# The mixing stage of a talking-heads attention and Fourier kernel: three engines in emission order, work dealt to steps by a table, maxima in halves, folding in small operations

## The chip, the cores and the metric

The kernel runs on one core of a Trainium2 chip. The metric is the device time of one execution in microseconds (us); lower is better. TensorE is called PE in the profile (its weight loads PEld), VectorE is DVE, ScalarE is ACT, GpSimd is POOL, SyncE is SP.

## The reference, cut to what matters

```python
scores = np.matmul(q, k.transpose(0, 1, 3, 2)) / np.sqrt(64)      # 8 batches, 12 heads, 448 x 448
scores = np.einsum('bhij,hg->bgij', scores, w_pre)                # premix: heads into heads
attn = np.exp(scores - np.max(scores, axis=-1, keepdims=True))
attn = attn / (np.sum(attn, axis=-1, keepdims=True) + 1e-09)
attn = np.einsum('bhij,hg->bgij', attn, w_post)                   # postmix
x = np.matmul(attn, v)          # then (8, 448, 12 * 64) = (8, 448, 768)
X = np.fft.fft(np.fft.fft(x, axis=1), axis=2)
u = x + np.real(X)
un = (u - mean(u)) / np.sqrt(var(u) + 1e-6)
out = u + np.maximum(un @ w_ch1, 0.0) @ w_ch2                     # 768 -> 3072 -> 768
```

Everything up to `u` is the mixing stage. The last two lines are the second stage; the change doesn't touch it.

## The kernel before

The mixing stage is a loop of 192 steps, 24 for each batch. A step mixes the heads of some twenty query rows (448 / 24 = 18.7). Its fixed part is the premix (eight matrix products, four for each half of its tile), a maximum, two exponentials, a scaling, the postmix and the transposition `Pv` of its result ("the turn"). Beside that, steps carry other products: scores of later rows (QK), attention times value (AV), transposes of q and k, transposes of x, and the two Fourier transforms of the previous batch (`emit_z`, `emit_s2`). These come from queues, `fill`, in which each entry has a step at which it is due.

```python
def emit_premix(T):
    mx = pmx.tile([P, 2, 512], F32, name="mx", tag="mx")      # one buffer, two PSUM banks
    ...                                                       # 4 products into half 0, 4 into half 1
def emit_max(T):                                              # VectorE: one maximum over both halves
    nc.vector.tensor_reduce(nmx[:, :], steps[T]["mx"][:, :, :S], axis=AX.X, op=ALU.max, negate=True)
def emit_exp(T):                                              # ScalarE
    for x in range(2):
        nc.scalar.activation(PP[:, x, :], steps[T]["mx"][:, x, :S], ACTF.Exp,
                             bias=steps[T]["nmx"][:, x:x + 1], accum_out=den[:, x:x + 1])
def emit_scale(T):                                            # GpSimd, with a reciprocal on VectorE
    nc.gpsimd.tensor_scalar(den[:, :], den[:, :], 1e-9, None, op0=ALU.add)
    nc.vector.reciprocal(out=rcp[:, :], in_=den[:, :])
    for x in range(2):
        nc.gpsimd.tensor_scalar(PP[:, x, :], PP[:, x, :], rcp[:, x:x + 1], 1.0, op0=ALU.mult, op1=ALU.mult)
def emit_turn(T):                                             # VectorE: transposes what postmix left in po
    nc.vector.transpose(g["Pv"]..., steps[T]["po"][:, :, :S])
...
# emit_s2, second transform: its product goes to one of four PSUM buffers `ms`;
# four VectorE additions to X then read that buffer and set it free
...
def fold(g):                                                  # GpSimd, for each pair of row groups
    nc.gpsimd.tensor_tensor(xs[:n, :], Xa[:n, :], Xb[:n, :], op=ALU.add)
    nc.gpsimd.tensor_tensor(xd[:n, :], Xa[:n, :], Xb[:n, :], op=ALU.subtract)
    ...                                                       # xe from xs, xo from xd: inputs of emit_z
...
with tc.manual_schedule(engines={mybir.EngineType.PE, mybir.EngineType.DVE}):
    while s < TOT or any(fill.values()):
        take("none", s)                                       # loads
        emit_premix(s + LM); emit_max(s + LM); emit_exp(s + LM)      # LM = 2
        flush()                                               # evacuations left from the step before
        take("tile", s)                                       # AV and QK products, between premix and postmix
        emit_postmix(s)
        ... wts.deal(1)                                       # one weight conversion on VectorE, in most steps
        emit_turn(s)
        emit_scale(s + LM)
        emit_gather(s + LG)                                   # SyncE: gathers Kr from the scores Sb, LG = 4
        take("full", s)                                       # transposes, transforms
        s += 1
```

`manual_schedule` names the engines whose instructions keep the order in which they are emitted. On the others the framework's scheduler chooses. PSUM evacuations were dealt to ScalarE or VectorE by a running estimate of each one's load (`_Evac`).

Of the kernel before, what the change touches and what calls it, by code (L numbers as in the profile page):

```python
# [61 lines left out]

NC = 6
# [47 lines left out]


class _Evac:


    def __init__(self, nc):
        self.nc = nc
        self.a = 0.0
        self.d = 0.0

    def pick(self, n):
        ca, cd = 165.0 + n * 0.833, 150.0 + n * 1.042
        if self.a + ca <= self.d + cd:
            self.a += ca
            return "a"
        self.d += cd
        return "d"

    def copy(self, out, in_, n):
        if self.pick(n) == "a":  # L130
            self.nc.scalar.copy(out=out, in_=in_)  # L131
        else:
            self.nc.vector.tensor_copy(out=out, in_=in_)

    def negate(self, out, in_, n):
        if self.pick(n) == "a":
            self.nc.scalar.mul(out, in_, -1.0)
        else:
            self.nc.vector.tensor_scalar(out, in_, -1.0, None, op0=ALU.mult)

    def relu(self, out, in_, n):
        if self.pick(n) == "a":
            self.nc.scalar.activation(out, in_, ACTF.Relu)
        else:
            self.nc.vector.tensor_scalar(out, in_, 0.0, None, op0=ALU.max)
# [127 lines left out]
def mix_phase(ctx, tc, ident, q, k, v, w_pre, w_post, u_scr, wts):  # L273
# [8 lines left out]
    praw = pool("praw", 3)  # L282
# [18 lines left out]
    ev = _Evac(nc)  # L301
    pend = []
# [45 lines left out]
    def emit_load_qk(b, xx):  # L348

        for nm, src in (("q", q), ("k", k)):  # L350
            t = praw.tile([P, C7, 2, D], F32, name="raw" + nm, tag="raw")
            for y in range(2):
                for x in range(2):
                    nc.gpsimd.dma_start(
                        out=t[64 * y:64 * y + 64, :, x, :],
                        in_=src[b, 6 * y + 2 * xx + x].rearrange(
                            "(p c) d -> p c d", c=C7))
            batches[b]["raw" + nm, xx] = t
        return []

    def emit_load_v(b):
        t = pvv.tile([P, 6, C7 * D], F32, name="vv", tag="vv")
        for y in range(2):
            nc.gpsimd.dma_start(
                out=t[64 * y:64 * y + 64, :, :],
                in_=v[b, 6 * y:6 * y + 6].rearrange("h (p c) d -> p h (c d)", c=C7))
        batches[b]["v"] = t
        return []


    def emit_xpose(b, xx, nm):
# [10 lines left out]
        for c0, n in ((0, 4), (4, 3)):  # L382
# [11 lines left out]
            evs.append(lambda dst=dst, src=src, n=n: ev.copy(dst, src, n * P))  # L394
        return evs

    def emit_qk(n, xx):
# [7 lines left out]
        for y in range(2):  # L405
            lo = r0 + MG * y
            for x in range(2):
# [5 lines left out]
        return [lambda x=x: ev.copy(bk["Sb"][:124, 2 * xx + x, :], pss[x][:124, :S], S)  # L413
                for x in range(2)]
# [24 lines left out]
    def emit_max(T):  # L439
        nmx = psm.tile([P, 2], F32, name="nmx", tag="nmx")  # L440
        nc.vector.tensor_reduce(nmx[:, :], steps[T]["mx"][:, :, :S], axis=AX.X,  # L441
                                op=ALU.max, negate=True)
        ev.d += 1084.0
        steps[T]["nmx"] = nmx

    def emit_exp(T):
# [6 lines left out]
        ev.a += 1656.0  # L453
        steps[T]["PP"], steps[T]["den"] = PP, den

    def emit_scale(T):
        PP, den = steps[T]["PP"], steps[T]["den"]
        nc.gpsimd.tensor_scalar(den[:, :], den[:, :], 1e-9, None, op0=ALU.add)
        rcp = psm.tile([P, 2], F32, name="rcp", tag="rcp")
        nc.vector.reciprocal(out=rcp[:, :], in_=den[:, :])  # L460
        ev.d += 150.0
# [17 lines left out]
    def emit_turn(T):  # L479
# [7 lines left out]
        ev.d += 1084.0  # L487
        steps[T].clear()

    def emit_av(g, pr):  # L490
# [6 lines left out]
        for jb in range(C7):  # L497
            for x in range(2):
                for y in range(2):
# [3 lines left out]
                        st["v"][64 * y:64 * y + 64, i, jb * D:(jb + 1) * D],  # L503
# [9 lines left out]
        def done(y):  # L513
            rs = _row(pss[y])
            eng = ev.pick(160 + 60)
            for e in range(2):
# [5 lines left out]
                if eng == "a":  # L522
                    nc.scalar.copy(out=dst, in_=src)
                else:
                    nc.vector.tensor_copy(out=dst, in_=src)
        evs = [lambda y=y: done(y) for y in range(2)]
        if pr == 2 and back:

            o = MG if g["gi"] == 1 else MG + GR
            evs.append(lambda: nc.gpsimd.memset(XT[:, :, o:o + 1], 0.0))  # L530
        pend.extend(evs)
        return []

    def emit_x(g):
# [5 lines left out]
        for u in range(2):  # L540
            ps = ms_tile()
            for i in range(3):
                nc.tensor.transpose(ps[:n, i * P:(i + 1) * P],
                                    XT[:, 3 * u + i, MG:MG + n], ident[:, :])
            evs.append(lambda u=u, ps=ps: ev.copy(X[:n, u * DH:(u + 1) * DH],
                                                  ps[:n, :DH], DH))
        if g["gi"] % 2:
            evs.append(lambda: fold(g))
        return evs

    def fold(g):
# [4 lines left out]
        xs = pxs.tile([GR + 1, DM], F32, name="xs", tag="xs")  # L556
        xd = pxs.tile([GR + 1, DM], F32, name="xd", tag="xd")
        nc.gpsimd.tensor_tensor(xs[:n, :], Xa[:n, :], Xb[:n, :], op=ALU.add)
        nc.gpsimd.tensor_tensor(xd[:n, :], Xa[:n, :], Xb[:n, :], op=ALU.subtract)
        xe = pxf.tile([GR + 1, DH + 1], F32, name="xe", tag="xe")  # L560
        xo = pxf.tile([GR + 1, DH - 1], F32, name="xo", tag="xo")
        nc.gpsimd.tensor_copy(out=xe[:n, 0:DH + 1:DH], in_=xs[:n, 0:DH + 1:DH])
        nc.gpsimd.tensor_tensor(xe[:n, 1:DH], xs[:n, 1:DH], xs[:n, DM - 1:DH:-1],
                                op=ALU.add)
        nc.gpsimd.tensor_tensor(xo[:n, :], xd[:n, 1:DH], xd[:n, DM - 1:DH:-1],
# [400 lines left out]
```

## Time and profile before

| | before |
|---|---|
| time, median of 3 (range) | 2651.92 us (2649.42 to 2665.38) |
| span of the profiled run, mean granted clock | 2652.4 us, 0.980 |
| first premix product | 46.77 us |
| from there to the first product of step 189 | 950.4 us |
| the rest (last steps, second stage) | 1655.2 us |

The page's first part gives busy time, share of the span and number of instructions of each engine:

```profile
PE 2454.0 (93%) x18544; PEld 1575.4 (59%) x18544; DVE 1514.2 (57%) x2842; ACT 723.5 (27%) x1989; POOL 660.0 (25%) x1129
```

Two lines of the waits were not used in the prediction; here they are for 200 to 900 us. The columns of a list of waits are: engine, its line and what it makes, whom it waited for; then us in total, times, longest us.

```profile
DVE Pv L484 <- PE po L473: 95.0, 67, 4.3
...
DVE rcp L460 <- POOL den L458: 72.8, 43, 4.8
```

VectorE stood 95 us at the turn, waiting for the postmix to end, and 72.8 us at the reciprocal, waiting for GpSimd to add 1e-9 to the sums `den`. VectorE is not the busiest engine, so both lines look harmless. The timeline tells them apart, by what they do to the next maximum. Count over batches 1 to 6, 144 steps. In 41 of them the turn, after a wait, began only 0.18 us after the next premix had begun, and still the maximum began 1.26 us after that premix on average, where 1.13 is usual: the late turn cost 0.13. But 33 maxima began more than 1.4 us after their premix, and before 29 of them VectorE's last wait was the one at the reciprocal. One of these steps begins with its premix at 393.18 and lasts 5.22 us, for 4.09 of products:

```profile
395.76 0.17 DVE L460 RECIPROCAL rcp<-den 128x2 f32<-128x2 f32 x1 [1.50 <-POOL den L458]
395.84 1.07 DVE L441 TENSOR_REDUCE nmx<-mx 128x2 f32<-128x896 f32 x1
...
398.40 1.15 PE L434 MATMUL mx<-Kr,kw 60*64 60x448 f32 x8 [1.05 <-ACT PP L450]
```

The bracket is idle time before, and what ended it. GpSimd made the sum late, the reciprocal held the maximum, the maximum the exponentials, and these the next premix. Where the next premix followed the exponentials at once (within 0.35 us), steps with this wait lost 29.4 of the 97.6 us that these six batches lose. The change moves that addition to VectorE.

### The profile page before, as it was taken

How to read it: one execution, taken by the hardware profiler on the slowest of the kernel's cores; microseconds unless marked ns; L12 is line 12 of the kernel's file. 1: busy time of each engine (PE TensorE's matmuls, PEld its weight loads, DVE VectorE, ACT ScalarE, POOL GpSimd, SP SyncE). 2: the span in 40 equal slices, each digit the busy share in tenths (PEclk: the TensorE clock that was granted, in tenths of full speed). 3: DMA queues.
4: the chain of work that ended last, by engine and by line, in shares of the span. 5: the costliest groups of instructions: out<-in, count | busy, mean ns of one | idle time of the engine just before them, and what ended most of it. 6: DMA issues, size and time to landing. Idle time of an engine off the chain costs nothing.

```text
span 2652.4 us, 47290 instructions
## 1 busy us (share of the span) xinstructions
PE 2454.0 (93%) x18544; PEld 1575.4 (59%) x18544; DVE 1514.2 (57%) x2842; ACT 723.5 (27%) x1989; POOL 660.0 (25%) x1129
## 2 busy tenths in 40 slices
PE   4889899899999885988899999999999999999999
PEld 2344444444444343665677777777777777777776
DVE  2666666666666664677646654665566356733333
ACT  2655555555555541211111111111111111111111
POOL 5565555556565532111000000000000000000000
PEclk8989999999999997999999999999999999999999
DMA  5453545444444433823264445443545354454331
GB/s 154 137 148 125 153 125 158 136 139 153 139 149 143 143 123 110 284 93 136 83 206 125 137 145 174 131 149 103 182 140 160 128 161 127 138 164 131 119 119 55
DMA packets 154141, 372.99 MB, mean 141 GB/s; under 512 B 21959, under 2 KB 75207, under 8 KB 153920
## 3 DMA queue, kind: packets, MB, share of 16 engines
q1 hardware_dynamic: 123360, 260.63, 29.8%
q0 software_dynamic: 30560, 109.34, 14.2%
q8 instruction: 148, 2.42, 0.4%
q14 instruction: 73, 0.60, 0.1%
HBM read 212.96 MB, written 74.34 MB: 108 GB/s over the span
## 4 chain that ended last, share of the span: by engine, by line
PE 74%; DVE 9%; POOL 5%; DMA 4%; ACT 3%; issue 2%; SPq 1%; POOLq 0%; ACTq 0%; DVEq 0%
PE psP L818 16%; PE psP L867 15%; PE psR L818 8%; PE psR L867 7%; PE mx L434 4%; PE psQ L818 4%; PE ms L501 4%; PE po L473 4%; PE psQ L867 4%; PE ms L408 3%; DMA Kr<-Sb 2%; PE ms L589 2%; ACT PP L450 2%; DVE nmx L441 2%; PE ms L575 2%
## 5 line engine op out<-in xcount | busy, mean ns | idle before, releaser
L867 PE MATMUL psP<-w2t,h 128*128 128x384 f32 x1344 | 464.2, 489 | 1.9 <-DVE u L873 1.9
L818 PE MATMUL psP<-ub,w1t 128*128 128x256 f32 x2016 | 463.5, 379 | 0.0
L818 PEld LDWEIGHTS psP<-ub,w1t 128*128 128x128 f32 x2016 | 383.1, 190 | 61.0 <-ACT ub L793 0.3
L867 PEld LDWEIGHTS psP<-w2t,h 128*128 128x128 f32 x1344 | 255.6, 191 | 170.5 <-DVE u L873 3.7
L450 ACT ACTIVATE PP<-mx,nmx 128x448 f32<-128x448 f32 x384 | 239.9, 629 | 408.2 <-DVE nmx L441 404.8
L202 POOL DMA_DIRECT2D raw<-in_moe_w_ch_dram x120 | 69.3, 577 | 923.6 <-DVE tmp L241 904.7
L484 DVE STREAM_TRANSPOSE Pv<-po 128x896 f32<-128x896 f32 x192 | 213.6, 1112 | 131.7 <-PE po L473 131.2
L463 POOL TENSOR_SCALAR PP<-PP,rcp 128x448 f32<-128x448 f32 x384 | 246.4, 652 | 132.3 <-DVE rcp L460 124.7
L441 DVE TENSOR_REDUCE nmx<-mx 128x2 f32<-128x896 f32 x192 | 207.5, 1081 | 119.4 <-PE mx L434 118.1
L873 DVE TENSOR_TENSOR u<-u,psP 128x384 f32<-128x384 f32 x336 | 182.5, 553 | 144.5 <-PE psP L867 141.9
L434 PE MATMUL mx<-Kr,kw 60*64 60x448 f32 x1536 | 198.0, 574 | 49.0 <-ACT PP L450 34.2
L823 ACT COPY h<-psP 128x512 f32<-128x512 f32 x42 | 24.6, 585 | 767.9 <-PE psP L818 767.9
L818 PE MATMUL psR<-ub,w1t 128*128 128x256 f32 x1008 | 231.3, 379 | 0.0
L867 PE MATMUL psR<-w2t,h 128*128 128x384 f32 x672 | 230.5, 486 | 0.0
L408 PE MATMUL ms<-kT,qT 64*64 64x448 f32 (+1 forms) x1536 | 205.4, 554 | 12.0 <-DVE X L602 11.3
L818 PEld LDWEIGHTS psR<-ub,w1t 128*128 128x128 f32 x1008 | 191.5, 190 | 26.0
L829 DVE TENSOR_TENSOR h<-h,psQ 128x512 f32<-128x512 f32 x42 | 28.9, 688 | 299.5 <-PE psQ L818 293.8
L501 PEld LDWEIGHTS ms<-Pv,vv 64*64 64x64 f32 x5376 | 161.0, 136 | 62.3 <-issue 37.1
L473 PE MATMUL po<-PP,kw 60*32 60x448 f32 x3072 | 193.6, 562 | 2.8 <-DVE rcp L460 2.3
L501 PE MATMUL ms<-Pv,vv 64*64 64x120 f32 x5376 | 172.5, 271 | 15.8 <-ACT Sb L131 15.4
L867 PEld LDWEIGHTS psR<-w2t,h 128*128 128x128 f32 x672 | 127.2, 190 | 87.4
L131 ACT COPY Sb<-ms 124x448 f32<-124x448 f32 x296 | 146.9, 537 | 32.9 <-DMA Kr<-Sb 12.6
(93 smaller groups left out, 2685.1 us busy)
## 6 DMA issues: line engine op xcount, KB each, us to landing
ub<-ub SPq DMA_DIRECT2D x294, 384.0 KB
Kr<-Sb SPq DMA_DIRECT2D x768, 105.0 KB
raw<-in_moe_w_ch_dram POOLq DMA_DIRECT2D x72, 256.0 KB, 3.2
raw<-in_moe_w_ch_dram POOLq DMA_DIRECT2D x48, 384.0 KB, 3.9
w<-wst POOLq DMA_DIRECT2D x18, 896.0 KB, 4.7
w<-wst POOLq DMA_DIRECT2D x12, 1344.0 KB, 6.3
w1t<-w SPq DMA_DIRECT2D x42, 384.0 KB
w2t<-w SPq DMA_DIRECT2D x42, 384.0 KB
```

The lines of the kernel that those rows point to most:

```text
L131: self.nc.scalar.copy(out=out, in_=in_)
L408: nc.tensor.matmul(pss[x][64 * y:64 * y + r0 + 64 - lo, :S], st["qT", xx][64 * x:64 * x + 64, y, lo:r0 + 64], st["kT", xx][64 * x:64 * x + ...
L434: nc.tensor.matmul(mx[64 * z:64 * z + 64, x, :S], kw1[64 * x:64 * x + KR, :], Kr[64 * x:64 * x + KR, z, :], start=True, stop=True)
L441: nc.vector.tensor_reduce(nmx[:, :], steps[T]["mx"][:, :, :S], axis=AX.X, op=ALU.max, negate=True)
L450: nc.scalar.activation(PP[:, x, :], steps[T]["mx"][:, x, :S], ACTF.Exp, bias=steps[T]["nmx"][:, x:x + 1], accum_out=den[:, x:x + 1])
L463: nc.gpsimd.tensor_scalar(PP[:, x, :], PP[:, x, :], rcp[:, x:x + 1], 1.0, op0=ALU.mult, op1=ALU.mult)
L473: nc.tensor.matmul(po[o:o + 32, z, :S], kw2[64 * z:64 * z + KR, y, :], PP[64 * z:64 * z + KR, :, c * HS:(c + 1) * HS], start=True, stop=True)
L484: nc.vector.transpose(g["Pv"][:, T % GT, :].rearrange("p (z s) -> p z s", z=2), steps[T]["po"][:, :, :S])
L501: nc.tensor.matmul(pss[y][64 * x:64 * x + 64, :nu * R], st["v"][64 * y:64 * y + 64, i, jb * D:(jb + 1) * D], _ap(Pv, 64 * y * rp + 32 * jb ...
L818: nc.tensor.matmul(p[:, m, :], w1[i][:, kc, m * P:(m + 1) * P], ub[:, kc, :], start=i in OPENS and m == kc == 0, stop=kc == NK - 1, skip_g ...
L867: nc.tensor.matmul(p, lhs[i][:, kf, x * P:(x + 1) * P], w2[i][:, kf, :], start=i in OPENS and kf == 0, stop=kf == FM - 1, skip_group_check ...
L873: nc.vector.tensor_tensor(us_, us_, p, op=ALU.add)
```

## The change

Its intent is that PE never waits in a full batch. PE, VectorE and ScalarE keep emission order. A table says at which step each piece of extra work comes. AV products move behind the postmix, QK products behind the scaling. The maximum is taken half by half, so that the first exponential can start early. GpSimd's folding is cut into six small operations, one a step, and the addition of 1e-9 goes to VectorE. Who evacuates what is fixed (`ENG`).

```diff
+AT_T = ((7, 0), (18, 18), (15, 17))
+AT_QK = ((0, 2, 2), (0, 1, 2), (0, 1, 2), (0, 1, 2),
+         (0, 1, 2), (1, 1, 2), (0, 1, 2), (0, 1, 2))
+AT_AV = ((0, 2, 4), (0, 1, 4), (3, 4, 5), (2, 3, 4))
+AT_X = (11, 20, 25, 29)
+AT_Z = (38, 38, 38, 38, 42, 42, 42)
+AT_S = ((41, 44), (49, 53))
+ENG = {("tr", "q", 4): "d", ("tr", "q", 3): "a", ("tr", "k", 4): "a",
+       ("tr", "k", 3): "d", "QK": "aa", "AV": "aa", "X": "aa", "z": "a"}
 ...
-    praw = pool("praw", 3)
+    praw = pool("praw", 4)
 ...                                  # q and k loaded one at a time, v in three parts
     def emit_max(T):
-        nc.vector.tensor_reduce(nmx[:, :], steps[T]["mx"][:, :, :S], axis=AX.X,
-                                op=ALU.max, negate=True)
+        for x in range(2):
+            nc.vector.tensor_reduce(nmx[:, x:x + 1], steps[T]["mx"][:, x, :S],
+                                    axis=AX.X, op=ALU.max, negate=True)
 ...
     def emit_scale(T):
-        nc.gpsimd.tensor_scalar(den[:, :], den[:, :], 1e-9, None, op0=ALU.add)
-        nc.vector.reciprocal(out=rcp[:, :], in_=den[:, :])
+        nc.vector.tensor_scalar(rcp[:, :], den[:, :], 1e-9, None, op0=ALU.add)
+        nc.vector.reciprocal(out=rcp[:, :], in_=rcp[:, :])
 ...
+        folds.extend([lambda: pairs(ALU.add, 0), lambda: pairs(ALU.add, 1), even,
+                      lambda: pairs(ALU.subtract, 0), lambda: pairs(ALU.subtract, 1),
+                      odd])
 ...
-    with tc.manual_schedule(engines={mybir.EngineType.PE, mybir.EngineType.DVE}):
+    with tc.manual_schedule(engines={ET.PE, ET.DVE, ET.Activation}):
         while s < TOT or any(fill.values()):
             take("none", s)
             if 0 <= s + LM < TOT:
                 emit_premix(s + LM)
                 emit_max(s + LM)
+            flush()
+            if 0 <= s + LM < TOT:
                 emit_exp(s + LM)
-            flush()
-            take("tile", s)
             if 0 <= s < TOT:
                 emit_postmix(s)
-                if s >= 4 and s % GS not in (13, 19, 0, 1):
-                    wts.deal(1)
+            take("AV", s)
+            if 0 <= s < TOT:
                 emit_turn(s)
+            if s >= 4:
+                wts.deal(1)
             if 0 <= s + LM < TOT:
                 emit_scale(s + LM)
+            if folds:
+                folds.pop(0)()
+            take("QK", s)
             if 0 <= s + LG < TOT:
 ...
                 emit_gather(s + LG)
             take("full", s)
             s += 1
```

## The prediction

> **What bounds the kernel now.** I read the page first, then the busy times by stretch, then step lengths from the timeline, then the waits and the chain of the mixing stage. The page says TensorE (PE) is busy 93% of 2652.4 us. That figure mixes two stages. In the stretches of the mixing stage (0 to about 1000 us) PE shows 85 to 93 busy us per 100; after 1400 us it shows 1200.00 busy in 1200. The second stage is not touched by the change and has nothing to give except at its start. So the question is the mixing stage: 192 steps, 24 for each of 8 batches.
>
> A step begins with the first premix product (line 434). The timeline of one step that runs tight (523 to 528 us) and of one that does not (532 to 538 us) shows what PE work costs and what waits cost. First the chain of waits there, whose pieces are time from piece to piece and so show throughput without pipeline tails (start, duration, what):
> ```profile
> 523.27 0.75 PE ms L408 x8
> 524.02 0.91 PE po L473 x16
> 524.93 2.78 PE ms L589 x8
> 527.71 0.91 PE mx L434 x8
> ...
> 530.29 2.13 PE ms L589 x6
> ...
> 543.68 1.52 PE ms L501 x51
> ```
> So, when PE is fed: premix 0.91, postmix 0.91, score products 0.75 us (2.57 for the three, needed in nearly every step), attention-times-value products 1.52, second transform 2.78 (even) or 2.13 (odd). By the same reading two first transforms take 1.72 (0.86 each) and six X transposes 0.91; steps with two sets of seven input transposes last 4.61 to 4.66, so one set is (4.66 - 2.57)/2, about 1.06 us. Steps with score and value products need 2.57 + 1.52 = 4.09, and the tight ones last 4.06 to 4.10. Now the one that does not (timeline; the bracket is idle time before, and who ended it):
> ```profile
> 532.35 0.98 PE L434 MATMUL mx<-Kr,kw 60*64 60x448 f32 x8
> ...
> 533.48 1.09 DVE L441 TENSOR_REDUCE nmx<-mx 128x2 f32<-128x896 f32 x1 [0.69 <-PE mx L434]
> ...
> 535.87 0.55 DVE L602 TENSOR_TENSOR X<-X,ms 112x383 f32<-112x383 f32 x1
> ...
> 536.48 0.97 PE L408 MATMUL ms<-kT,qT 64*64 64x448 f32 x6 [0.93 <-DVE X L602]
> ...
> 538.29 0.98 PE L434 MATMUL mx<-Kr,kw 60*64 60x448 f32 x8
> ```
> It lasts 538.29 - 532.35 = 5.94 for the same 4.09 of products: two score products stood in the queue because their PSUM tile was still being added to X by VectorE (DVE), which first had to do the maxima of this step. The lost 1.85 is more than the bracketed 0.93, because products already started are counted busy while they drain.
>
> I did this for all steps from the first premix (46.77 us) to 997: they last 950 us, their products need 803, so 147 us are lost. Six full batches (1 to 6) last 730 in place of 634: 121.7 against 105.7 each, 16 lost. The losses sit in fixed places of the 24: step 13 (3.3 us, value products waiting for ScalarE (ACT) evacuations), 5 (2.8), 19 (2.5), 6 (1.75), 1 (1.5), 18 (1.1), 21 (0.9). Steps with little beside the basic products last 3.71 to 3.82 for up to 3.48 of work: there the loop premix, maximum, exponentials, next premix bounds, since the premix tile has one buffer. The waits between 200 and 1000 us agree:
> ```profile
> DVE nmx L441 <- PE mx L434: 87.9, 73, 3.4
> ...
> PE mx L434 <- ACT PP L450: 20.5, 32, 2.0
> ...
> PE ms L501 <- ACT Sb L131: 15.4, 7, 2.2
> ...
> PE ms L385 <- ACT Sb L131: 13.3, 11, 5.2
> ...
> PE ms L408 <- DVE X L602: 11.3, 11, 1.4
> ```
> **What the Trainium skill says.** "Perfetto Trace Analysis", Identifying the Most-Contended Engine, calls matmul busy share a bad measure of headroom because matmuls are pipelined; this trace agrees, PE reads as 91% busy in a batch (110.58 of 121.20 us from 347.04 to 468.24) whose products need 105.7/121.2 = 87%. "TensorE: Matmul & The Clock Gate", head table, gives ScalarE and VectorE strictly first-in-first-out queues: the order of emission decides what waits, which is how the 5.94 us step came about. "PSUM — Partial Sum Buffer", PSUM bank collisions, forbids two engines in one bank at once; the two halves of the premix tile are 512 floats each, a bank each, so a maximum of half 0 beside products of half 1 is allowed (before, one maximum reads both, so no trace shows it yet). "SBUF — State Buffer", Who interferes with whom, says that VectorE's two-port modes and GpSimd exclude each other; the trace agrees: the 128x256 mask of line 219 took 0.28 us at 74.63 and 1.08 at 540.54, while GpSimd scaled from 540.22 for 1.25. One such conversion a step stays as it was.
>
> **The change part by part.**
> *Work.* PE products are the same, 105.7 us a batch. Maxima in halves: 24 x 1.09 becomes 48 of some 0.55, no more than 1 us a batch. The 1e-9 addition moves from GpSimd (0.215 each) to DVE (about 0.1 each). All evacuations except half of the input transposes go to ACT: 24 x 2 of 0.45, value copies 12 x 0.5, X 8 x 0.4, z 7 x 0.31, inputs about 4, with 24 x 1.24 of exponentials, some 67 us of 106. DVE has about 80 us. Neither becomes the bound on average.
> *The loop premix to premix.* It is 3.76 to 3.82 now. The first exponential waits for 0.54 less, so about 3.2; if the first half may start before the second half's products, 2.8. The table leaves no step of a full batch below 3.32 us of products (I summed each of the 24: 3.32 to 4.09 for most, 5.6 to 6.5 in steps 1, 5, 14, 17, 18, 20). So in a full batch PE sets the pace in each step and the loop has slack.
> *PSUM waits.* Every second transform is now followed in its step by transposes, whose emission flushes its four DVE additions before the next maxima. In step 1: transform over at 5.35, additions (4 x 0.47, plus 0.2) at 7.45, next maximum due at 6.26 + 1.1 = 7.36, value products at 8.08. Practically no wait where 1.85 was lost. Steps 13, 18, 19 lose their waits the same way (3.3, 1.1, 2.5), as does the exponential wait in 21 and 22.
> *GpSimd.* Folding in pieces of 0.9 to 1.3 us, one a step, replaces runs of 1.82 + 1.80 + 0.18 + 1.0 + 1.0. But steps 9 to 11 hold three loads of four issues (0.73 each, 8.8) plus scaling 3 x 1.25 plus folding about 3, or 15.5 us against 10.9 of PE: it falls behind by about 4.6, and the scaling has about 3.6 of slack before its postmix. I charge 1 to 2 us a batch for that.
> *Sum.* Batches 1 to 6: 3.5 lost in place of 16, from all residues; 6 x 12.5 = 75. Batches 0 and 7, which lack products to fill with and lose 19 and 24: 8 and 10, saves 25. The four steps around the start: 5 less. Together about 105.
> *Ends.* The first premix waits until 46.77 with 10.4 us for its gather; four input buffers in place of three and fewer loads ahead of it: 5 us less, an estimate with little under it. At the end PE waits 6.63 for the fold and then SyncE for the weight store:
> ```profile
> 1044.59 6.79 DMA w<-wst
> ...
> 1053.64 6.38 DMA u<-u
> ```
> Conversions are now dealt in every step from 4 on (188 for 160 operations, where 158 were dealt before), so the store is long done: up to 6.8 saved if the final write of X doesn't take its place, and 3 to 4 from even folds first. I take 8.
> Total 105 + 5 + 8 = 118, so 2534. I give back 11 for what the sums cannot see, and predict 2545.
>
> **Rivals.**
> (1) GpSimd takes over: it is busy 70.5 of 121.2 us in the batch above; squeezed into 107 us and with loads bunched it may hold up postmix more than I charged. For: chain pieces on folding and scaling already exist (xs 1.82, xd 1.78). Against: pieces are now small. Worth 3 to 5 us a batch: 2570 to 2580.
> (2) The gathers (Kr): SyncE issues four of 0.767 a step, 3.07 of 4.4 us, and the score buffer waits for them to land (ACT waited 4.61 at 308 to 313 us). For: pace rises by 12%. Against: evacuations into it now come a step later, and PE waited for gathers only 8.9 us from 200 to 1000. If it binds: 2580 to 2600.
> (3) Strict order on ACT puts evacuations ahead of the exponentials of the same step and stalls when one is late. Against: these evacuate products issued before the premix. If wrong in the full steps: gain halves, 2595.
> (4) Nothing new binds and losses vanish: 803 plus some 15, 2505.
>
> **Range and chances.** Because product times are fixed to about 0.03 us a step, the floor is firm: 2500. The upside of the time is open to (1) to (3), singly likely mild. Range 2505 to 2598. Faster by over 2% means below 2599: 0.91. Within 2%: 0.08. Slower: 0.01.
>
> **What would show it.** Steps with value and score products at 4.09 nearly everywhere; batch period 107 to 111; second stage unchanged (36.2 us a tile in the steady part); products waiting for X additions or Sb copies close to gone; no w store on the chain at the end. Wrong if batches last over 115: then PE waits, read before postmix (GpSimd), before premix (gathers or exponentials), or before value products (ACT order), tell which rival it is.

## The result, and the profile after

| | before | after |
|---|---|---|
| time, median (range), 4 runs each | 2654.11 us (2649.42 to 2665.38) | 2546.99 us (2544.47 to 2549.62) |
| span and clock of the profiled run | 2652.4 us, 0.980 | 2542.7 us, 0.991 |
| first premix product | 46.77 us | 49.14 us |
| from there to step 189 | 950.4 us | 844.8 us |
| the rest | 1655.2 us | 1648.8 us |
| a full batch (mean of 1 to 6), of it lost | 121.68, 16.35 | 108.07, 3.20 |
| lost in batch 0, batch 7 | 19.4, 24.1 | 13.2, 6.3 |

The ratio is 0.9591, with a 95% interval of 0.9557 to 0.9624. A ratio here is the mean time of one kernel's runs over the mean of the other's in the same rounds, so it isn't quite the ratio of the medians. The three parts of the profiled spans add up: +2.4 - 105.6 - 6.4 = -109.7 us, the difference of the spans. "Lost" is the length of a step less what its products need when fed, summed; the needs are good to some 0.1 us, and step 18 reads 0.68 too little in every kernel with the new table.

First the page of the kernel after:

```profile
PE 2418.8 (95%) x18544; PEld 1552.7 (61%) x18544; DVE 1522.3 (60%) x3159; ACT 769.7 (30%) x2056; POOL 638.0 (25%) x1001
```

PE runs the same 18544 products. Its busy time fell by 35 us although its work didn't change: most of that must be stalls inside products, and some may be a slower clock (below). In the pages' fifth parts a half maximum costs 619 ns where one over both halves cost 1081, so the pair is dearer.

The chain around a second transform (start, duration, what), the place that stalled score products before:

```profile
552.58 0.91 PE po L460 x16
553.49 0.91 PE ms L397 x8
554.40 2.78 PE ms L582 x8
557.18 0.77 PE ms L374 x7
557.94 0.91 PE mx L423 x8
```

PE goes from one product to the next without a piece of any other engine in between. That step, from its premix at 551.63 to the next at 557.87, takes 6.24 us, where the single costs of before sum to 6.41. Step after step of the full batches reads like this. The timeline of the same moment shows why nothing waits:

```profile
557.21 0.56 DVE L593 TENSOR_TENSOR X<-X,ms 112x385 f32<-112x385 f32 x1 [1.42 <-PE ms L582]
...
558.61 0.55 DVE L595 TENSOR_TENSOR X<-X,ms 112x383 f32<-112x383 f32 x1
...
559.08 1.15 DVE L431 TENSOR_REDUCE nmx<-mx 128x1 f32<-128x448 f32 x2
```

The additions that free the transform's PSUM buffer begin the moment it ends and are over before VectorE takes the next maxima. Before, they came after the maximum, and the buffer stayed taken.

The waits of the kernel after from 200 to 900 us, the lines that answer to those of before:

```profile
PE po L460 <- POOL PP L450: 7.4, 12, 1.3
PE mx L423 <- ACT PP L439: 7.3, 16, 1.8
...
PE ms L397 <- DVE kT L283: 6.0, 6, 1.0
...
DVE Pv L471 <- PE po L460: 2.3, 5, 1.1
```

Score products no longer wait for additions to X, nor value products for evacuations of the scores. What is left is a postmix waiting for GpSimd's scaling, and a score product in step 19 waiting for an evacuation of kT. VectorE's 95 us at the turn have become 2.3, and no line with a reciprocal that waits for GpSimd is left.

And the chain at the join of the stages:

```profile
938.93 3.44 DMA u<-X,rows
```

The store of a weight tile is gone from the chain. The last write of X now stands in its place.

The parts of step time lost, by step of the batch (mean over batches 1 to 6):

| step | before | after |
|---|---|---|
| 13 (value products for evacuations) | 3.29 | about 0 |
| 5 | 2.81 | about 0 |
| 19 | 2.46 | 1.10 |
| 6, 1 | 1.75, 1.54 | about 0 |
| 18, 21 | 1.06, 0.94 | below 0, about 0 |
| 8, 23 (postmix for GpSimd) | not among the largest | 0.93, 0.59 |

One thing besides the waits differs. The granted clock of the kernel after is 1.00 in each of the eight batches; that of the kernel before is 1.00 in batches 3 and 4 alone, and 0.95, 0.97, 0.96, 0.99, 0.97 and 0.92 in batches 0, 1, 2, 5, 6 and 7. Batches 3 and 4 lose 14.4 and 13.5 us, batches 1, 2, 5 and 6 18.6, 19.8, 16.8 and 14.4. So a part of the gain may be the clock's, some 2 us a full batch (an estimate: the mean of the six, 16.3, less that of batches 3 and 4, 14.0). No run separates it, or shows why the clock differs.

### The profile page after: what moved, and what is told of

It reads as the page before. It is cut to its first block, busy times and chain, and to the rows that moved or that the text cites. A ratio compares the mean times of both kernels' runs of the same rounds, so it can differ in the third digit from the quotient of the medians.

```text
span 2542.7 us, 47627 instructions
## 1 busy us (share of the span) xinstructions
PE 2418.8 (95%) x18544; PEld 1552.7 (61%) x18544; DVE 1522.3 (60%) x3159; ACT 769.7 (30%) x2056; POOL 638.0 (25%) x1001
## 4 chain that ended last, share of the span: by engine, by line
PE 81%; DVE 7%; POOL 5%; DMA 3%; ACT 2%; issue 2%; SPq 0%; ACTq 0%; POOLq 0%; DVEq 0%
PE psP L821 17%; PE psP L870 16%; PE psR L821 9%; PE psR L870 8%; PE mx L423 5%; PE ms L487 5%; PE psQ L821 4%; PE po L460 4%; PE ms L397 4%; PE psQ L870 4%; PE ms L582 3%; DVE nmx L431 2%; ACT PP L439 2%; PE ms L568 2%; POOL xs L545 2%
## 5 line engine op out<-in xcount | busy, mean ns | idle before, releaser
L431 DVE TENSOR_REDUCE nmx<-mx 128x1 f32<-128x448 f32 x384 | 221.5, 619 | 163.2 <-PE mx L423 162.8
L450 POOL TENSOR_SCALAR PP<-PP,rcp 128x448 f32<-128x448 f32 x384 | 240.8, 639 | 284.6 <-DVE rcp L448 228.1
L397 PE MATMUL ms<-kT,qT 64*60 64x448 f32 (+1 forms) x1536 | 186.8, 557 | 7.6 <-DVE kT L283 7.6
L283 ACT COPY Sb<-ms 124x448 f32<-124x448 f32 x384 | 184.2, 541 | 7.4 <-PE ms L397 5.3
L487 PEld LDWEIGHTS ms<-Pv,vv 64*64 64x64 f32 x5376 | 142.8, 132 | 69.0 <-issue 27.1
L487 PE MATMUL ms<-Pv,vv 64*64 64x120 f32 x5376 | 165.0, 268 | 0.0
```

Of the source, the lines that this page charges most:

```text
L283: (nc.scalar.copy if eng == "a" else nc.vector.tensor_copy)(out=out, in_=in_)
L397: nc.tensor.matmul(pss[x][64 * y:64 * y + r0 + 64 - lo, :S], st["qT", xx][64 * x:64 * x + 64, y, lo:r0 + 64], st["kT", xx][64 * x:64 * x + ...
L431: nc.vector.tensor_reduce(nmx[:, x:x + 1], steps[T]["mx"][:, x, :S], axis=AX.X, op=ALU.max, negate=True)
L487: nc.tensor.matmul(pss[y][64 * x:64 * x + 64, :nu * R], st["v", pr][64 * y:64 * y + 64, x, jb * D:(jb + 1) * D], _ap(Pv, 64 * y * rp + 32 ...
```

## The experiments

The theory going in: PE paces the steps after the change, and the gain comes from PSUM buffers freed in time, which needs both the table (what comes when) and the order (who does what first). The rivals: the halves of the maximum give the gain; the small folding operations do; or the fixed order of one engine alone does. A rival that was not tested is the move of the 1e-9 addition off GpSimd: every variant of the kernel after keeps it. Twelve kernels ran, all correct, each with 3 rounds; the kernel before ran beside them.

### The maxima: e1, e2, e3

e1 takes one maximum over both halves again:

```diff
-        for x in range(2):
-            nc.vector.tensor_reduce(nmx[:, x:x + 1], steps[T]["mx"][:, x, :S], axis=AX.X, op=ALU.max, negate=True)
+        nc.vector.tensor_reduce(nmx[:, :], steps[T]["mx"][:, :, :S], axis=AX.X, op=ALU.max, negate=True)
```

> The changed kernel with one maximum over both halves, as before the change. Theory A (the halves bought nothing: in the trace of the changed kernel the first exponential starts at 72.60, after both halves have ended at 72.49, and the loop of a lean step is 3.79 us as before): time within 4 us of the changed kernel's 2547, lean steps 3.72 to 3.82. Theory B (the halves shorten the loop by 0.5 as predicted, something else takes it back): lean steps go to 4.2 or more, total up by 15 us or more.

Measured: 2546.49 us (2544.84 to 2549.82), ratio 0.957 (0.9543 to 0.9598), the same as the kernel after. The halves gave nothing. The timeline of a step with little work in the kernel after shows it:

```profile
73.99 0.98 PE L423 MATMUL mx<-Kr,kw 60*64 60x448 f32 x8 [0.99 <-ACT PP L439]
...
75.12 1.16 DVE L431 TENSOR_REDUCE nmx<-mx 128x1 f32<-128x448 f32 x2 [0.71 <-PE mx L423]
...
76.39 0.64 ACT L439 ACTIVATE PP<-mx,nmx 128x448 f32<-128x448 f32 x1 [1.59 <-DVE nmx L431]
```

The first maximum starts when all eight premix products are through, and the first exponential starts at 76.39, after both maxima (75.12 + 1.16 = 76.28). Splitting an operation doesn't split the wait. But which wait? e2 gives the two results tiles of their own:

```diff
-        nmx = psm.tile([P, 2], F32, name="nmx", tag="nmx")
+        nmx = [psm.tile([P, 1], F32, name=f"nmx{x}", tag=f"nmx{x}") for x in range(2)]
...                                  # and the two places that use it
```

> The two halves of the maximum write two tiles in place of two columns of one. Theory A (the wait of the first exponential is on the tile that both maxima write): the first exponential starts about 0.55 earlier, lean steps go from 3.79 to about 3.2; sum of what lean steps lose: some 1.4 us a batch, 8 in the first and last: total down 12 to 20 us, to about 2530. Rival (ScalarE is held by what stands before the exponential in its queue, not by the maximum): lean steps stay at 3.79, total within 4 us.

Measured: 2549.66 us (2547.54 to 2550.36), ratio 0.9583 (0.9555 to 0.9611). No gain, so the shared tile of results was not what held the exponential. e3 also splits the premix tile itself, which lies in two PSUM banks, into two tiles of one bank:

```diff
-        mx = pmx.tile([P, 2, 512], F32, name="mx", tag="mx")
+        mx = [pmx.tile([P, 512], F32, name=f"mx{x}", tag=f"mx{x}") for x in range(2)]
```

> As the run with two maximum tiles, and the premix tile is two tiles of one bank each. Theory: the first maximum starts about 0.4 earlier, when its own half of the products is done, and the next step's first half of products may start after the first exponential; lean steps about 2.8, near their product time; total 2522 to 2530, some 5 below the run with two maximum tiles alone. Rival: PE sets the pace once the loop is 3.2, no more than 2 us below it.

Measured: 2533.54 us (2529.75 to 2537.21), ratio 0.9523 (0.9493 to 0.9553): some 13 us less than the kernel after by the medians. In its timeline an exponential now stands between the two maxima:

```profile
78.14 0.62 DVE L431 TENSOR_REDUCE nmx<-mx 128x1 f32<-128x448 f32 x1
...
78.86 0.63 ACT L439 ACTIVATE PP<-mx,nmx 128x448 f32<-128x448 f32 x1 [0.53 <-DVE nmx L431]
...
79.12 0.62 DVE L431 TENSOR_REDUCE nmx<-mx 128x1 f32<-128x448 f32 x1 [0.35 <-PE mx L423]
```

The second half of this premix had waited for a gather, which drew the two maxima apart. But over batches 1 to 6 the first exponential starts 0.44 us before the second maximum ends, on average, where in the kernel after and in e2 it starts 0.12 after. The waits of the compiled programs say the same. In e2 the first exponential of a step carries a wait on VectorE and PE and the second carries none, so the first one's wait must cover both maxima. In e3 each exponential has its own wait on VectorE:

```
e2:
78 L439 Activation PP,den<-mx,nmx_1181 128x448 [waits DVE_49,PE_49,Pool_49]
79 L439 Activation PP,den<-mx,nmx_1182 128x448
e3:
78 L439 Activation PP,den<-mx_1191,nmx_1197 128x448 [waits DVE_49,Pool_49]
79 L439 Activation PP,den<-mx_1192,nmx_1198 128x448 [waits DVE_49]
```

So the framework orders the accesses of two engines to a PSUM tile by the tile, not by the half or the bank.

### Table and order: e5, b1, e9, e6, e7

e5 keeps all of the kernel after, with the steps of the kernel before in the table (four of the seven first transforms one step later):

```diff
+AT_T = ((5, 5), (16, 17), (17, 18))
+AT_QK = ((0, 1, 2),) * 8
+AT_AV = ((1, 2, 3),) * 4
+AT_X = (10, 16, 22, 28)
+AT_Z = (31, 31, 32, 33, 34, 35, 35)
+AT_S = ((36, 42), (47, 48))
```

> The changed kernel's order of emission with the step table of before (first transforms moved by at most two steps, because the folding in pieces ends later). Theory T (the table makes most of the gain, by putting transposes behind each second transform and value products where there is room): full batches last 114 to 119 in place of 108, total 2600 to 2640. Rival O (the fixed order on the three engines makes it): full batches at 111 or less, total below 2575.

Measured: 2608.65 us (2599.99 to 2611.66), ratio 0.9823 (0.9794 to 0.9852). A full batch lasts 116.66 us and loses 11.3.

b1 goes the other way: the kernel before, with its order, and the new table. It loads q and k one at a time, but keeps three input buffers and loads v whole, since a fourth buffer didn't fit in SBUF there.

```diff
-            due("full", f + aq, lambda b=b, xx=xx: emit_xpose(b, xx, "q"))
+                due("full", f + a - GS, lambda b=b, xx=xx, nm=nm: emit_xpose(b, xx, nm))
...
-                due("tile", f + GT * n + GT + 1 + pr, lambda g=g, pr=pr: emit_av(g, pr))
+                due("tile", f + GT * (n + 1) + AT_AV[n][pr], lambda g=g, pr=pr: emit_av(g, pr))
```

> The kernel before with the new step table alone (inputs loaded one by one with three buffers, old order of emission, old evacuation balance, folding in one run, one maximum). Theory T (the table makes most of the gain): total 2570 to 2600, full batches 110 to 113. Rival O (the order makes it, and a table without it is worth little): total 2620 or more, full batches 117 or more.

Measured: 2622.82 us (2617.35 to 2628.05), ratio 0.9866 (0.9836 to 0.9896). Its waits from 200 to 900 us:

```profile
DVE Pv L491 <- PE po L480: 127.9, 74, 8.5
...
PE ms L508 <- DMA vv<-in_v_dram: 15.7, 6, 3.4
```

The second line is a flaw of the experiment: with the new table the whole-v load comes too late for the value products of step 6, where 5.3 us a batch are lost, 38.8 in all. So b1 understates what the table alone can give. As measured, the table alone gives 1.3%, the rest of the change 1.8%, together 4.1%. That this is more than the sum of the two isn't shown, since the flaw hides up to 1.5% (an estimate from the 38.8 us). By the expectation's own numbers b1 fell on the side of rival O, and e5 on that of theory T: neither part alone gives the gain. Steps 13, 5, 1 and 21, which lost 3.29, 2.81, 1.54 and 0.94 before, lose nothing in b1, so the table alone is enough for what was lost there. The rest of b1's loss, 12.4 us a batch, lies above all in steps 22 and 23 (3.1 and 1.6). In step 22 of all six full batches the maximum comes late behind the reciprocal, which waits for GpSimd as it did before.

The first line is the turn again, at 128 us. In b1 it does little: once in 144 steps was it the last wait before a late maximum.

e9 keeps everything after and only puts AV and QK products back between premix and postmix:

```diff
-            if 0 <= s < TOT:
-                emit_postmix(s)
             take("AV", s)
+            take("QK", s)
             if 0 <= s < TOT:
+                emit_postmix(s)
                 emit_turn(s)
```

> The changed kernel with value and score products between premix and postmix, as before, all else as changed. Theory (PE is the pace in full batches and every buffer has slack, so the place in the step hardly counts): within 8 us of 2547. Rival (the products at the end give the scaling and the evacuations time; earlier they stand in front of the postmix and wait for PSUM): full batches at 110 or more, total up 15 or more.

Measured: 2599.80 us (2597.35 to 2602.28), ratio 0.9787 (0.9758 to 0.9816). That is 53 us more than the kernel after by the medians, as much as half of the whole gain. I had expected hardly anything of it. The timeline of a step of e9 that lasts 5.48 us (190.09 to 195.57) in place of its 3.6 of products:

```profile
190.09 0.98 PE L423 MATMUL mx<-Kr,kw 60*64 60x448 f32 x8
190.27 1.12 DVE L471 STREAM_TRANSPOSE Pv<-po 128x896 f32<-128x896 f32 x1 [2.03 <-PE po L460]
...
192.93 1.13 DVE L431 TENSOR_REDUCE nmx<-mx 128x1 f32<-128x448 f32 x2
...
194.18 0.64 ACT L439 ACTIVATE PP<-mx,nmx 128x448 f32<-128x448 f32 x1 [2.91 <-DVE nmx L431]
```

VectorE works in emission order, and the turn of a step stands ahead of the maximum of the next. With the products in front of it the postmix ends late, the turn waits (2.03 idle), and then the maxima start 2.84 us after the premix, where 1.1 is usual (73.99 to 75.12 above). The exponentials are late by that, and so is the next premix, which needs the one premix tile free. In e9's waits from 200 to 900 us VectorE stands 150.4 us at the turn, and PE 42.7 us before the premix (7.3 in the kernel after). With the postmix directly behind the premix, the turn's data is ready while the AV and QK products still run. The step is no exception: of 70 maxima that come late in batches 1 to 6 (over 1.4 us after their premix), 69 have the wait at the turn as VectorE's last.

But e9 isn't the order of before. There a late turn cost the maximum 0.13 us, because only the reciprocal stood between the two; the weight conversion stood ahead of the turn, in the time of its wait. Since the change the conversion stands behind the turn. In 57 steps of e9 a turn that waited until after the next premix had begun is followed by a conversion (0.48 us on average), the addition of 1e-9 and the reciprocal, and the maximum begins 2.01 us after the premix, 0.88 later than usual. In the step above the addition alone took 0.97 us (at 191.84), as GpSimd folded beside it. So the 53 us are what the early postmix is worth in the new order of VectorE, and not a loss that the kernel before had. No run put the conversion back ahead of the turn.

e6 emits the second transform after the transposes of its step, not before them:

```diff
-    def due(kind, at, fn):
-        fill[kind].append((at, len(fill[kind]), fn))
+    def due(kind, at, fn, late=0):
+        fill[kind].append((at, len(fill[kind]) + late, fn))
...
-                    lambda b=b, pair=pair, par=par: emit_s2(b, pair, par))
+                    lambda b=b, pair=pair, par=par: emit_s2(b, pair, par), 10000)
```

> The changed kernel with each second transform after the transposes of its step in place of before them, so that its additions are emitted after the next maxima. Theory (the PSUM tile that the additions hold is what stopped PE before): in the steps after a second transform (2, 6, 18, 21 of 24) 0.5 to 2 us lost each where 0 is lost now, 3 to 6 a batch, total up 25 to 50, to 2570 to 2597. Rival (with the new order PE has slack there and the place does not matter): within 5 us of 2547.

Measured: 2578.58 us (2577.4 to 2579.67), ratio 0.9705 (0.9677 to 0.9732), 32 us more than the kernel after. Its timeline at an odd transform:

```profile
365.69 2.20 PE L582 MATMUL ms<-tdo,z 128*112 128x385 f32 x6 [0.59 <-ACT Sb L283]
...
368.94 1.16 DVE L431 TENSOR_REDUCE nmx<-mx 128x1 f32<-128x448 f32 x2 [3.26 <-PE mx L423]
...
370.01 0.55 DVE L593 TENSOR_TENSOR X<-X,ms 112x385 f32<-112x385 f32 x1
```

The transform first waits 0.59 for one of the four PSUM buffers. Then its additions come behind the maxima, 2.1 us after it ended (365.69 + 2.20 = 367.89), and the buffer is held so long that three score products of step 21 slip into the next step. The same table, the same products, one exchange in the order of emission, and full batches lose 8.98 us in place of 3.20.

e7 takes ScalarE out of the fixed order:

```diff
-    with tc.manual_schedule(engines={ET.PE, ET.DVE, ET.Activation}):
+    with tc.manual_schedule(engines={ET.PE, ET.DVE}):
```

> The changed kernel with ScalarE ordered by the scheduler again in place of by emission. Theory (fixed order on ScalarE counts only where evacuations stood behind an exponential that was not ready, as in step 13 of before, 2.2 us): losses of 1 to 3 us in some steps return, total up 10 to 40. Rival 1 (no part in the gain): within 4 us. Rival 2 (emission order holds exponentials back): total down.

Measured: 2550.79 us (2549.76 to 2552.49), ratio 0.9604 (0.9577 to 0.9631); the interval overlaps that of the kernel after. ScalarE's fixed order is no visible part of the gain.

### GpSimd: e4, e8, e11

e4 emits all six fold operations at once:

```diff
-        folds.extend([lambda: pairs(ALU.add, 0), ..., odd])
+        six = [lambda: pairs(ALU.add, 0), lambda: pairs(ALU.add, 1), even,
+               lambda: pairs(ALU.subtract, 0), lambda: pairs(ALU.subtract, 1), odd]
+        folds.append(lambda: [f() for f in six])
```

> All six pieces of a fold emitted at once instead of one a step. Theory (GpSimd's order isn't fixed by emission; its trace in the changed kernel shows the six pieces back to back anyway, 573.97 to 580.75, with no scaling between): total within 5 us of the changed kernel, the postmix waits in steps 8 and 23 of a batch unchanged (0.9 and 0.6 us). Rival (the pieces do help): losses at those steps grow to 2 us or more each, total up 15 us or more.

Measured: 2552.63 us (2544.17 to 2559.26), ratio 0.9585 (0.9553 to 0.9617): not told apart from the kernel after, though its full batches lost 4.8 us in the profile. The reason is in the kernel after itself. This is GpSimd's part of its timeline:

```profile
573.97 1.96 POOL L545 TENSOR_TENSOR xs<-X 112x384 f32<-112x384 f32 x2 [0.24 <-ACT X L283]
...
580.75 1.04 POOL L602 DMA_INDIRECT u<-X,rows  x1 [0.16 <-issue]
581.84 2.48 POOL L450 TENSOR_SCALAR PP<-PP,rcp 128x448 f32<-128x448 f32 x4
```

The pieces are emitted one a step but run back to back: GpSimd isn't among the engines of fixed order, and the compiled program has all six in a row, with the indirect write of X behind them and two steps' scaling behind that. The cut into small operations hardly took effect. e8 makes it take effect, by putting GpSimd into the fixed order:

```diff
-    with tc.manual_schedule(engines={ET.PE, ET.DVE, ET.Activation}):
+    with tc.manual_schedule(engines={ET.PE, ET.DVE, ET.Activation, ET.Pool}):
```

> The changed kernel with GpSimd in order of emission too, so that the pieces of a fold do stand one a step between the scalings. Theory (the pieces help only with a fixed order): the postmix waits in steps 8 and 23 of a batch (0.9 and 0.6 us) go, total down 5 to 10. Rival (fixed order puts four-issue loads, and row-indexed writes that wait for X and for another write, ahead of scalings): new postmix waits of 2 us or more in the steps with loads or after odd second transforms, total up 10 to 60.

Measured: 2609.21 us (2606.16 to 2612.25), ratio 0.9825 (0.9796 to 0.9855), 62 us more than the kernel after. One of its waits from 200 to 900 us:

```profile
POOL u L602 <- DMA u<-X: 49.8, 8, 7.2
```

In emission order the indirect write of X comes right after the plain write of X on SyncE's queue, and waits until that has landed, up to 7.2 us, with all scaling behind it. PE then loses 5.4 us in each step 12 on average. So GpSimd's free order is better than this emission order: the scheduler had moved that write.

e11 starts from e10 (below) and does the folding on VectorE, one piece a step:

```diff
-            nc.gpsimd.tensor_tensor(box[-1][:n, h], Xa[:n, h], Xb[:n, h], op=op)
+            nc.vector.tensor_tensor(box[-1][:n, h], Xa[:n, h], Xb[:n, h], op=op)
...                                  # and the other three calls of the fold
```

> Starts from the kernel with two premix tiles and early flush (2531.03 us median), and moves the ten fold additions, subtractions and two small copies of each batch from GpSimd to VectorE, one piece a step in VectorE's fixed order. If GpSimd's unordered fold pieces, run back to back ahead of the scaling, are what is left in steps 8 and 23 (1.43 and 1.03 us a batch there), those losses go: about 2.3 us a batch, eight batches, so 2513 us (2508 to 2520); full batches average 104.8 in place of 107.0, and products waiting for the scaled PP disappear from the waits. At the end the last fold gets shorter too, perhaps 2 us of these. Rival: VectorE is now the delay. It was busy 74 of 107 us there; twelve pieces of about 0.5 us (an estimate from the 0.55 us of an addition of 112x383 that it does for the second transform) make 80 of 105, but a piece sits between the reciprocal and the next maximum in its queue, and could delay either: then the losses move to premix or score steps and the time stays at 2528 to 2540. A third possibility is that the scaling is late because its reciprocal is late, not because GpSimd is busy: then steps 8 and 23 keep their losses.

(The count in that text is off: a batch has twelve additions and subtractions and two small copies.) Measured: 2532.73 us (2530.08 to 2536.45), ratio 0.9556 (0.953 to 0.9582): no gain over e10. The expected 2.3 us a batch failed, and the trace says why, differently for the two steps. In step 8 the folding was a part of the cause: its mean loss falls from 1.43 to 0.70, and in the first full batch the wait is gone. But 0.54 and 0.37 us are now lost in steps 9 and 10, where a fold piece of 113x383 on VectorE ran 1.70 us (at 185.38) beside a scaling on GpSimd and held up the maxima; five pieces of 112x383 averaged 0.558. In step 23 the folding was not the cause (timeline):

```profile
247.34 1.35 POOL L602 DMA_INDIRECT u<-X,rows  x1 [8.09 <-DMA Kr<-Sb]
...
248.73 2.48 POOL L450 TENSOR_SCALAR PP<-PP,rcp 128x448 f32<-128x448 f32 x4
...
250.03 0.99 PE L460 MATMUL po<-PP,kw 60*32 60x448 f32 x16 [1.50 <-POOL PP L450]
```

GpSimd has nothing to compute and still stands idle for 8.09 us at the indirect write, while a reciprocal that was ready at 243.39 waits for its scaling until 248.73. In the kernel after, the folding ran during that time and hid it. What is left in step 23 is the place of that write in GpSimd's queue.

### An earlier flush: e10

e10 is e3 with the pending evacuations flushed before the maxima in place of after them:

```diff
                 emit_premix(s + LM)
-                emit_max(s + LM)
             flush()
             if 0 <= s + LM < TOT:
+                emit_max(s + LM)
                 emit_exp(s + LM)
```

> The run with two premix tiles, and pending evacuations emitted before the maxima in place of after them, so that the last quarter of a transposed k is copied before VectorE waits for the premix. Theory: the 1.0 us that score products lose in step 19 of every batch for that copy goes, 7 to 9 us in all: about 2525. Rival (the wait moves to the gather or to the exponentials): 2531 to 2537, as without it.

Measured: 2531.03 us (2523.98 to 2535.59), ratio 0.952 (0.9486 to 0.9553). Against e3's 0.9523 that is no difference. In the profile, step 19's loss of 1.02 us a batch is gone, since the score product there no longer waits for kT, but 0.5 us of it come back in step 8. e3, e10 and e11 are faster than both given kernels, and can't be told apart from one another by their times.

| kernel | first premix | to step 189 | full batch | lost in it | batch 0, 7 lost |
|---|---|---|---|---|---|
| after | 49.14 | 844.8 | 108.07 | 3.20 | 13.2, 6.3 |
| e3 | 47.19 | 836.9 | 107.24 | 2.37 | 15.1, 3.6 |
| e10 | 47.00 | 836.2 | 107.00 | 2.13 | 16.6, 3.6 |
| e11 | 46.45 | 832.5 | 106.84 | 1.97 | 12.4, 4.2 |
| e9 | 48.92 | 899.1 | 115.60 | 10.73 | 18.1, 9.7 |
| e8 | 40.93 | 913.4 | 117.86 | 12.99 | 19.8, 8.8 |

## Why the prediction was right, and where it wasn't

The time came out 2 us from the predicted one, and the sum of the steps too. Not all of its terms were right.

- **The floor and the losses: right.** Products cost the same in both kernels, and full batches lose 3.2 us where 3.5 was said, with a period of 108.07 where 107 to 111 was to be seen. Steps with value and score products last 4.0 to 4.1 nearly everywhere. From the first premix to step 189 the gain is 105.6, and 105 was said. The rivals that needed a slower pace (gathers, ScalarE's order) did not show: PE's waits for gathers in the full batches are small, and e7 says that ScalarE's order hardly matters.
- **PSUM waits: the mechanism is right, and it isn't all.** e6 shows that the place of the second transform ahead of transposes is worth 32 us. But "Steps 13, 18, 19 lose their waits the same way" doesn't fit steps 18 and 19. Their maxima came 2.8 and 2.9 us late, and in 11 of these 12 steps behind the reciprocal that waited for GpSimd. That wait stood in the prediction's own view of 200 to 1000 us, with 83.9 us, and was not used. The prediction booked the move of the 1e-9 addition as work alone; it takes this wait away, and what that is worth was not measured by itself. Nor does the prediction name the place of the postmix, worth 53 us in the new order (e9). It took the losses of each step as waits for buffers and let them all vanish. It got the size because it summed what was lost, not what removed it, and that is luck in part.
- **Busy share.** "This trace agrees" with "Perfetto Trace Analysis" holds for the conclusion and not for the direction. The page says that pipelined PE instructions look smaller in the trace; here the share, 91%, was larger than the 87% that the products need.
- **"The first exponential waits for 0.54 less, so about 3.2": wrong.** The loop from premix to premix stayed at 3.79. e1 shows that the halves give nothing, e2 and e3 that the premix tile is what ties the two halves together. I had argued from the banks, which would have allowed it, and not from the tile, on which the framework waits. It cost the sum little, since full batches have few steps with so little work. Batches 0 and 7 have more of them: 13.2 and 6.3 lost, where 8 and 10 was said; the sum, 19.5, is near 18. Both ran at a granted clock of 1.00 where before had 0.95 and 0.92, which is in their gain and can't be split off.
- **GpSimd: size right, place and cause wrong.** "I charge 1 to 2 us a batch for that" came out as 1.5, but in steps 8 and 23, not in the steps 9 to 11 of the loads. "Folding in pieces of 0.9 to 1.3 us, one a step" is what the source says and not what the compiled program does: the six pieces run in a row, and e4 shows that emitting them so changes nothing that the times can tell. For step 23 e11 shows the indirect write as the wait underneath.
- **The 1e-9 on VectorE: under-sized.** "about 0.1 each" is 0.229 on average in the trace. In the full batches of the kernel after, VectorE has room for it; what it saves was left out (see PSUM waits).
- **The head: wrong.** The first premix came 2.4 us later, not 5 earlier. Its wait for the gather was 10.4 and is 10.95. The estimate was said to have little under it, and no experiment was made on it. But e8 began at 40.93, with 2.86 us of waiting for the gather, so GpSimd's order has to do with it; how is open.
- **The end: 6.4 in place of 8.** The store of the weights left the chain, as said, and the final write of X took its place there, the caveat that was named. PE's wait for the fold fell from 6.63 to 3.39, as said.
- **The 11 us given back** cover the head's miss of 7.4 and the end's 1.6. They stood for no named cause, so that they fit is luck in part.

What stays open: how much of the table's worth is the table alone, as b1 had a late load of v; what the 1e-9 addition on VectorE gives alone, or what it would cost to put it back; what the fixed choice of evacuating engines (`ENG`) and the fourth input buffer give, which no run undid; the part of the clock; what it would bring to move the indirect write to another place in GpSimd's queue; and the head.

## What to carry to other kernels

When an engine with a fixed order holds both the end of one step (the turn) and the start of the next (the maximum), look at everything that stands between them in its queue. A turn that came late put off the maximum by 0.13 us where only a reciprocal that was ready stood between, and by 0.88 with a conversion and an addition there too; in that order an early postmix was worth 53 us. And look for a tiny operation that waits for another engine's full queue: one addition to 128x2 elements on GpSimd stood behind 29 of 33 late maxima. To overlap two halves of an operation, give each half a tile of its own, all the way through the chain, and look in the trace for an operation that starts between the two halves; if there is none, the split did nothing. Check in the trace that small operations which you meant to spread are in fact spread, as an engine outside the fixed order runs them as its scheduler likes.

## What the Trainium skill lacked or had wrong

- "PSUM — Partial Sum Buffer", PSUM bank collisions, says what may overlap by bank and 32-partition quadrant. That was not enough here. The waits of this kernel's framework are by PSUM tile: with one tile over two banks the exponential waited for both maxima (e2, 2549.66 us), with two tiles of one bank it didn't (e3, 2533.54 us). The page doesn't speak of waits by tile.
- "SBUF — State Buffer", Who interferes with whom, names VectorE operations with two SBUF inputs, and `tensor_scalar` in a two-port mode, as those that contend with GpSimd. The traces agree with the first (in e11 a 113x383 fold piece took 1.70 us beside GpSimd's scaling, and five of 112x383 averaged 0.558). What the page lacks is a figure for tiny operations: the addition of 1e-9 to 128x2 elements took 0.12 to 0.17 us alone, and 0.97 at 191.84 in e9, while GpSimd added two tiles.
- No page that I read says what an indirect write costs the computing queued behind it on GpSimd when it waits for another transfer: up to 7.2 us at a time in e8 and 8.09 us in e11.
